# Three more score blocks turned by DMA, keys turned two groups at a time, and a written table of extra products

## The chip, the cores and the metric

The kernel runs on one core of a Trainium2 chip. The metric is the device time of one launch in microseconds (us). Three runs of the kernel before gave a median of 765.36 us (765.35 to 765.82).

Five engines work side by side, each with its own queue of instructions in order. TensorE (PE, with its weight loads shown as PEld) multiplies matrices and writes the result to PSUM. VectorE (DVE), ScalarE (ACT) and GpSimd (POOL) work on elements. SyncE (SP) only issues DMAs here: loads of `u`, stores of the output, and all transposes that the DMA engines make ("turns").

## The reference

For each of 8 batches, with S = 3200 tokens, D = 256, and 64 columns in `z`, `w_q` and `w_k`:

```
scores = (z @ z.T) / S                 # S x S, symmetric
attn   = max(scores, 0) ** 2           # symmetric too
x      = u * (attn @ v)                # S x D
q, k   = x @ w_q, x @ w_k              # S x 64
mixed  = (q @ k.T / 8) @ x             # S x D
out    = max(mixed, 0) @ w_out
```

The kernel computes `mixed` as `q @ (k.T @ x) / 8`; `k.T @ x` is the small matrix that the code calls "heads".

## The kernel before, in words

**Groups and tiles.** The 25 row tiles of 128 tokens of a batch are put into 7 groups: six of 512 tokens and a last one of 128 (`LASTG`). For each group, the transposed attention matrix is needed in blocks of 128 rows x 512 columns. One block is a score product (`scores`, L291: 64 rows of `z` against 512 columns), a first stage that scales and clamps it (`first_stage`, DVE at L305 or ACT at L303) and a second stage that squares it to fp16 (`second_stage`, POOL at L316 or ACT at L314). Blocks are made two at a time, as "score pairs": a pair fills one PSUM tile of 128 x 1024, its two matmuls use 64 rows of the array each and run side by side. Three such PSUM tiles exist (`pps`); mixes, output products and key projections use them too.

**Turned blocks.** `attn` is symmetric, so the block of groups (gi, gj) is the transpose of that of (gj, gi). Where `is_turned(gi, gj)` holds, the block is computed once, and a DMA transpose of the finished fp16 pair (`tt<-at`, issued by SP at L335) makes its mirror image. Before, ten blocks of a batch are turned: the neighbours up to two groups apart, and (0, 4). The mirror images live in seven buffers `tt0` to `tt6`, given out by a plan in which the one that comes free first is taken.

**Second product.** For each group, PE adds up `attn @ v` over all 25 row tiles in two PSUM banks, `acc0` and `acc1` (L353, 64 rows of the array per matmul in two lanes). There is one copy of these banks, so a new group's products can begin when the group before has been read out of them. That is done by `gate`: DVE multiplies one half by `u` (L491, into `x_sb`), ACT copies the other half out (L490, `gt`) and POOL multiplies it.

**Steps.** The order of all work is written by a loop over steps `k`, with three score pairs made in a step, or two and a mix. The step also takes some rows of the second product of the current group (`rows_`), which may be freshly made blocks of at least two steps ago (`LAG`) or mirror images that wait in `left`. A step that begins a group first issues a number of score pairs (`heading`) and then the group's products; the others are interleaved between the products at the shares in `shares_of`.

**Extra products.** A step can carry one of three kinds of extra work: a key step (`keys_and_heads`: project a group's `x` by `w_q` and `w_k`, copy the result out at L528, turn the keys by DMA, L535, and add up the heads of an earlier group), a mix (`mix`, L641: two matmuls of 512 columns, clamped on ACT at L662), and an output product (`project`, 16 matmuls of 256 columns, scaled on ACT at L723, stored by SP at L724). Which step carries which is decided by the rules `mix_due` and `key_due` and in the test for `projecting`, but for 15 steps that `chosen` sets by hand.

**What SP issues.** In order of the program: turns of `x` (`turn_x`, L502), loads of `u` (L179), turns of score pairs (L335), turns of keys (L535), of `z` for the next batch (`turn_z`, L160), and stores.

Of the kernel before, what the change touches and what calls it, by code (L numbers as in the profile page):

```python
# [16 lines left out]
def kernel(  # L17
# [15 lines left out]
    P = 128  # L33
# [155 lines left out]
    kxs = [pk.tile([P, 4, 2, dh], FP16, tag=f"kx{i}", name=f"kx{i}") for i in range(4)]  # L189
    raw = {}  # L190

# [34 lines left out]
    FOR_SMALL = (3, 4, 5)  # L226

# [40 lines left out]

    tt_of, tt_free = {}, [(-1.0, n) for n in range(7)]
    for b, gi, tis in tiles:  # L270
# [201 lines left out]
    def gate(b, gi):  # L472
        nn = widths[gi] // P
        if gi < LASTG:
            xs[b, gi] = px.tile([P, 4, D], FP16, tag="x_sb", name="x_sb")
        else:
            xs[b, gi] = px.tile([P, 1, D], FP16, tag="xl", name="xl", bufs=1)
        x = xs[b, gi][:].rearrange("p n d -> p (n d)")
        ug = us.pop((b, gi))[:].rearrange("p n d -> p (n d)")
# [16 lines left out]
    def turn_x(b, gi):  # L496
        nn = widths[gi] // P
        if gi < LASTG:
            xTs[b, gi] = pxt.tile([P, 4, ND, P], FP16, tag="xT_sb", name="xT_sb")
        else:  # L500
            xTs[b, gi] = pxt.tile([P, 1, ND, P], FP16, tag="xTl", name="xTl", bufs=1)
        nc.sync.dma_start_transpose(  # L502
            out=xTs[b, gi][:, 0:nn, :, :].rearrange("p n a s -> p (n a) s"),
            in_=xs[b, gi][:, 0:nn, :].rearrange("p n d -> p (n d)"),
        )


# [14 lines left out]
    def projections_out(b, gi, out):  # L522
        gw = widths[gi]
        if gi < LASTG:
            qks[b, gi] = pq.tile([P, W], FP16, tag="qk", name="qk")
        else:
            qks[b, gi] = pq.tile([P, P], FP16, tag="ql", name="ql", bufs=2)
        nc.scalar.copy(out=qks[b, gi][:, 0:gw], in_=out)  # L528

    def turn_keys(b, gi):  # L530
        gw = widths[gi]
        mine = slice(0, dh) if swapped(gi) else slice(dh, P)
        kxs.append(kxs.pop(0))
        ks[b, gi] = kxs[-1]
        nc.sync.dma_start_transpose(  # L535
            out=ks[b, gi][:, 0 : gw // P, 0, :],
            in_=qks[b, gi][mine, 0:gw],
        )

    def swapped(gi):  # L540
        return gi % 2 == 1 or gi == LASTG
# [237 lines left out]
    def between(k, fn):  # L779
        todo_between.append((k, fn))  # L780

    def group_done(k, b, gi):
        if gi < LASTG - 1:
            between(k + (5 if b + 1 < B else 3), lambda: keys_and_heads(b, [gi]))
        elif gi == LASTG and b + 1 < B:
            between(k + 5, lambda: keys_and_heads(b, [LASTG - 1, LASTG]))
# [10 lines left out]
    def keys_and_heads(b, gis):  # L797
# [5 lines left out]
        aside = None  # L803
        late = len(groups) <= NG
        heads_of = keyed[: late or len(keyed) == 2]
        if late and len(keyed) == 2 and keyed[0][0] == keyed[1][0]:
            heads_of = [(keyed[0][0], keyed[0][1] + keyed[1][1])]
            keyed[:2] = heads_of
        full = len(heads_of) == 1
# [22 lines left out]
        def after():  # L832
            for gi, o in zip(gis, outs):
                projections_out(b, gi, o)
                turn_keys(b, gi)
            if full:
                hb, hgis = keyed.pop(0)
                heads_out(hb, hgis, ps)
                if hgis[-1] == LASTG:
                    mixed_at[0] = max(mixed_at[0], now[0] - 1)  # L840
                    todo_mix.extend((hb, i, db) for i in range(LASTG // 2) for db in range(ND))
                    side.append((side_mix, side_mix_out, hb))
            if aside:
                aside[1](aside[2], ps)
            keyed.append((b, gis))
            keyed_at[0] = now[0]
# [3 lines left out]
    def group_begun(k, b, gi):  # L850
# [487 lines left out]
```

## Time and profile before

| | before |
|---|---|
| median of three runs | 765.36 us |
| the profiled execution | 765.27 us |
| its span, first to last instruction | 763.5 us |
| PE busy | 753.3 us (99%), 12888 matmuls |
| POOL, ACT, DVE busy | 545.3, 526.4, 462.0 us |
| mean granted clock of PE | 0.997 |
| packets of the DMA engines | 289613, 135.88 MB |

"Busy" is the time in which an engine has at least one instruction running. Matmuls overlap, and their ends are modelled, so PE's busy time is not by itself time at its peak rate. In a timeline row the first number is the start, the second the time from the first start to the last end of the merged instructions, and `x16` their count. A name like `SPq` is an engine's issuing of DMAs, which is not counted as busy.

### The profile page before, as it was taken

The numbers are of one execution on the slowest core, as the hardware profiler recorded it, in microseconds if no ns is written. First come the engines' busy times: TensorE is split into PE (matmuls) and PEld (weight loads), VectorE is DVE, ScalarE is ACT, GpSimd is POOL, SyncE is SP. The second block draws the span as 40 slices with busy tenths as digits, with TensorE's granted clock in tenths as the row PEclk, the third lists the DMA queues.
The fourth block names the chain that finished last, engine by engine and source line by source line (L and its number), as shares of the span: only waits on it lengthen the run. The fifth ranks groups of instructions, "written<-read, shape, count | busy, mean of one in ns | idle before, by whom it ended". The sixth has DMA issues, their size and how long they took to land.

```text
span 763.5 us, 28995 instructions
## 1 busy us (share of the span) xinstructions
PE 753.3 (99%) x12888; PEld 617.9 (81%) x12888; DVE 462.0 (61%) x458; ACT 526.4 (69%) x619; POOL 545.3 (71%) x383
## 2 busy tenths in 40 slices
PE   8999999999999999999999999999999999999996
PEld 6777888888888887888888888888878888888884
DVE  7654676546755567555665557655566565755534
ACT  8666676676767676676775867658676586776555
POOL 7988797678867688675888569966698665854540
PEclk9999999999999999999999999999999999999998
DMA  9999699997999979999999979999599995798636
GB/s 193 176 191 201 104 175 175 141 181 112 183 172 205 188 146 187 201 189 171 191 195 194 210 151 150 169 201 237 105 198 204 200 209 127 170 227 188 168 74 261
DMA packets 289613, 135.88 MB, mean 178 GB/s; under 512 B 265168, under 2 KB 269648, under 8 KB 289488
## 3 DMA queue, kind: packets, MB, share of 16 engines
q1 hardware_dynamic: 279696, 117.80, 80.2%
q0 software_dynamic: 9648, 15.98, 15.3%
q8 instruction: 100, 1.64, 0.9%
q14 instruction: 25, 0.20, 0.1%
q10 hardware_dynamic: 144, 0.26, 0.1%
HBM read 59.38 MB, written 26.21 MB: 112 GB/s over the span
## 4 chain that ended last, share of the span: by engine, by line
PE 97%; DVE 2%; ACT 1%; issue 0%; DVEq 0%; ACTq 0%
PE acc L353 72%; PE sc L291 12%; PE fo L353 5%; PE qk L353 5%; PE mx L641 1%; DVE x_sb L491 1%; DVE fo L1296 0%; PE sc L965 0%; DVE g L305 0%; ACT at L314 0%; ACT g L303 0%; PE qk L594 0%; PE xtx L618 0%; PE ztp L129 0%; PE hd L628 0%
## 5 line engine op out<-in xcount | busy, mean ns | idle before, releaser
L305 DVE TENSOR_SCALAR g<-sc 128x1024 f32<-128x1024 f32 x329 | 400.6, 1224 | 240.2 <-PE sc L291 228.5
L316 POOL TENSOR_TENSOR at<-g 128x1024 f16<-128x1024 f32 x229 | 432.3, 1897 | 123.9 <-DVE g L305 100.2
L353 PE MATMUL acc<-v_sb,at 64*128 64x256 f16 (+1 forms) x7187 | 462.0, 269 | 2.2 <-DVE x_sb L491 0.5
L353 PEld LDWEIGHTS <-at 64*128 64x128 f16 (+1 forms) x7187 | 353.9, 94 | 87.6 <-PE acc L353 25.3
L314 ACT ACTIVATE at<-g 128x1024 f16<-128x1024 f32 x227 | 236.2, 1055 | 19.3 <-DVE g L305 11.8
L353 PE MATMUL acc<-v_sb,tt 64*128 64x256 f16 x2552 | 178.7, 269 | 0.0
L303 ACT ACTIVATE g<-sc 128x1024 f32<-128x1024 f32 x127 | 130.0, 1023 | 55.3 <-PE sc L291 52.3
L291 PE MATMUL sc<-zT 64*128 64x512 f16 (+1 forms) x1008 | 164.7, 356 | 0.4 <-DVE zT L135 0.3
L353 PEld LDWEIGHTS <-tt 64*128 64x128 f16 x2552 | 130.2, 94 | 14.1
L493 POOL TENSOR_TENSOR x_sb<-gt,u_sb 128x512 f16<-128x512 f32 x48 | 61.2, 1274 | 64.5 <-ACT gt L490 60.1
L662 ACT ACTIVATE rt<-mx 128x1024 f16<-128x1024 f32 x47 | 47.9, 1024 | 32.7 <-PE mx L641 32.5
L490 ACT COPY gt<-acc 128x512 f32<-128x512 f32 x48 | 28.1, 585 | 49.9 <-PE acc L353 49.9
L291 PEld LDWEIGHTS <-zT 64*128 64x128 f16 x1008 | 51.8, 94 | 8.7 <-issue 1.5
L353 PE MATMUL fo<-wo,rt 64*128 64x256 f16 (+1 forms) x696 | 57.9, 270 | 0.0
L528 ACT CAST qk<-qk 128x512 f16<-128x512 f32 x47 | 27.5, 586 | 39.5 <-PE qk L353 36.9
L353 PEld LDWEIGHTS <-rt 64*128 64x128 f16 (+1 forms) x696 | 35.5, 94 | 15.3 <-PE fo L353 6.3
L491 DVE TENSOR_TENSOR x_sb<-acc,u_sb 128x512 f16<-128x512 f32 x48 | 33.2, 691 | 20.4 <-PE acc L353 19.2
L723 ACT ACTIVATE fo<-fo 128x1024 f32<-128x1024 f32 x39 | 39.9, 1024 | 1.9 <-PE fo L353 1.7
L353 PEld LDWEIGHTS <-x_sb 64*128 64x128 f16 x672 | 29.8, 95 | 4.5 <-PE qk L353 0.9
L353 PE MATMUL qk<-kx,x_sb 64*128 64x64 f16 x672 | 32.8, 190 | 0.0
L146 POOL DMA_DIRECT2D v_sb<-in_v_dram x49 | 28.7, 586 | 0.0
L353 PE MATMUL qk<-xT_sb,wkq 64*128 64x512 f16 (+3 forms) x118 | 25.7, 326 | 0.0
(84 smaller groups left out, 249.8 us busy)
## 6 DMA issues: line engine op xcount, KB each, us to landing
u_sb<-in_u_dram SPq DMA_DIRECT2D x48, 512.0 KB, 5.4
out_dram<-fo SPq DMA_DIRECT2D x43, 512.0 KB, 3.9
v_sb<-in_v_dram POOLq DMA_DIRECT2D x43, 256.0 KB, 5.2
tt<-at SPq DMA_TRANSPOSE x162, 5.1
out_dram<-fo SPq DMA_DIRECT2D x9, 256.0 KB, 2.9
zr<-in_z_dram POOLq DMA_DIRECT2D x7, 256.0 KB, 4.2
u_sb<-in_u_dram SPq DMA_DIRECT2D x8, 128.0 KB, 4.4
zr<-in_z_dram POOLq DMA_DIRECT2D x7, 144.0 KB, 6.4
```

Of the source, the lines that this page charges most:

```text
L146: nc.gpsimd.dma_start(out=vs[b][:, n0 : n0 + nn, :], in_=rows(v, b)[:, n0 : n0 + nn, :])
L291: nc.tensor.matmul(out=sc[:, h, at : at + w], lhsT=zT[b][half : half + dqk, ds(z_at(b, h) + ti * P, P)], rhs=zT[b][half : half + dqk, ds(z ...
L303: nc.scalar.activation(out=g[:], in_=sc[:], func=RELU, scale=GSCALE)
L305: nc.vector.tensor_scalar(out=g[:], in0=sc[:], scalar1=0.0, scalar2=GSCALE, op0=AOP.max, op1=AOP.mult)
L314: nc.scalar.square(out=out, in_=g[:])
L316: nc.gpsimd.tensor_mul(out=out, in0=g[:], in1=g[:])
L353: return nc.tensor.matmul(out=self.out, lhsT=self.lhsT(rows), rhs=self.rhs(rows), start=start, stop=stop)
L490: nc.scalar.copy(out=upper[:], in_=accs[1][:])
L491: nc.vector.tensor_mul(out=x[:, 0:n], in0=accs[0][:, 0:n], in1=ug[:, 0:n])
L493: nc.gpsimd.tensor_mul(out=x[:, n : 2 * n], in0=upper[:], in1=ug[:, n : 2 * n])
L662: nc.scalar.activation(out=out, in_=ps[:], func=RELU)
L723: nc.scalar.mul(out=flat_out[:, sl], in_=part, mul=FINAL_SCALE)
```

## The change

- `is_turned` holds for (0, 3), (1, 4) and (2, 5) too: 13 blocks of a batch are turned. Their mirror images are no longer computed. Ten buffers hold turned blocks instead of seven.
- To make room, `px` goes from 7 to 6 buffers, `pxt` from 4 to 3, `pq` from 11 to 6.
- Except in the last batch, the keys of an even group and the next odd group are put side by side in one tile `kp` of 128 partitions and are turned by one DMA; the 128-token group goes with the third pair. ACT copies the half with the queries, DVE the half with the keys (a new instruction). Heads can be added only after the pair is turned.
- `x` of the last two groups shares one tile `x5` and, except in the last batch, one DMA. The turn of `z` is cut in two DMAs (7 and 6 blocks) instead of three.
- A string `EXTRAS` sets for every step which extra product it carries: `k` a key step, `p` an output product, `m` a mix, `x` a mix and an output product, `.` none. The rules are used no more.

```diff
-    px = ctx.enter_context(tc.tile_pool(name="px", bufs=7))
+    px = ctx.enter_context(tc.tile_pool(name="px", bufs=6))
...
-    pxt = ctx.enter_context(tc.tile_pool(name="pxt", bufs=4))
+    pxt = ctx.enter_context(tc.tile_pool(name="pxt", bufs=3))
...
-    pq = ctx.enter_context(tc.tile_pool(name="pq", bufs=11))
+    pq = ctx.enter_context(tc.tile_pool(name="pq", bufs=6))
...
+    ALSO = ((0,3),(0,4),(1,4),(2,5))
+
     def is_turned(gi, gj):
-        return gi < gj < LASTG and (gj <= gi + FAR or (gi, gj) == (0, 4))
+        return gi < gj < LASTG and (gj <= gi + FAR or (gi, gj) in ALSO)
...
-    tt_of, tt_free = {}, [(-1.0, n) for n in range(7)]
+    tt_of, tt_free = {}, [(-1.0, n) for n in range(10)]
...
     def gate(b, gi):
         nn = widths[gi] // P
-        if gi < LASTG:
+        if gi < LASTG - 1:
             xs[b, gi] = px.tile([P, 4, D], FP16, tag="x_sb", name="x_sb")
-        else:
-            xs[b, gi] = px.tile([P, 1, D], FP16, tag="xl", name="xl", bufs=1)
...
+        elif gi == LASTG - 1:
+            xs[b, gi] = px.tile([P, 5, D], FP16, tag="x5", name="x5", bufs=1)
+        else:
+            xs[b, gi] = xs[b, gi - 1][:, 4:5, :]
...
     def projections_out(b, gi, out):
         gw = widths[gi]
...
+        pair = gi // 2
+        if gi % 2 == 0:
             qks[b, gi] = pq.tile([P, W], FP16, tag="qk", name="qk")
-        else:
-            qks[b, gi] = pq.tile([P, P], FP16, tag="ql", name="ql", bufs=2)
-        nc.scalar.copy(out=qks[b, gi][:, 0:gw], in_=out)
+            kps[b, pair] = pk.tile([P, W + P], FP16, tag="kp", name="kp", bufs=2)
+        else:
+            qks[b, gi] = qks[b, gi - 1]
+        q, k = (slice(dh, P), slice(0, dh)) if swapped(gi) else (slice(0, dh), slice(dh, P))
+        nc.scalar.copy(out=qks[b, gi][q, :], in_=out[q, :])
+        nc.vector.tensor_copy(out=kps[b, pair][k, 0:W], in_=out[k, :])
 
     def turn_keys(b, gi):
         gw = widths[gi]
...
+        if gi % 2 == 0 and gi < LASTG or gi == LASTG - 1:
+            return
+        pair = min(gi // 2, 2)
+        n = 5 if gi == LASTG else 4
+        kx = pk.tile([P, 5, 2, dh], FP16, tag="kp2", name="kx", bufs=2)
         nc.sync.dma_start_transpose(
-            out=ks[b, gi][:, 0 : gw // P, 0, :],
-            in_=qks[b, gi][mine, 0:gw],
+            out=kx[:, 0:n, :, :].rearrange("p n a h -> p n (a h)"), in_=kps[b, pair][:, 0 : n * P]
         )
...
-            keyed.append((b, gis))
+            if b == last:
+                keyed.append((b, gis))
+            elif gis[0] % 2 == 1:
+                keyed.append((b, [gis[0] - 1]))
+                keyed.append((b, gis))
...
-            for i, n0 in enumerate((0, 5, 9)):
-                due(k + (10 if b == 0 else 6) + i, lambda n0=n0: turn_z(b + 1, n0, 5 if n0 == 0 else 4))
+            for i, (n0, nn) in enumerate(((0, 7), (7, 6))):
+                due(k + (10 if b == 0 else 6) + i, lambda n0=n0, nn=nn: turn_z(b + 1, n0, nn))
...
-    heading_more = {165: -1}
-    chosen = {
-        18: "k", 19: "p", 20: "p", 21: "m", 35: "k", 36: "p", 38: "p", 101: "p", 142: "mp",
-        147: "k", 148: "m", 149: "m", 159: "mp", 161: "p", 163: "m"
-    }
+    heading_more = {}
+    EXTRAS = (
+        "..............k.k..k.k...k.k.k..k...mk.mkpmkmpm.kpk.p.k.mkmkmppkmmkpkpkppkmm"
+        "kpkpmmkppkmmkmmkppmkpmpkmpkmk..pkmk.mkpkpmpmppmkpkmkmpkxkxxkxkxkxxkxxxxkxk.k"
+        "."
+    )
+    chosen = {k: "mp" if c == "x" else c for k, c in enumerate(EXTRAS)}
```

More of the change, by code (lines that the diff above doesn't have):

```diff
@@ L189 @@
     kxs = [pk.tile([P, 4, 2, dh], FP16, tag=f"kx{i}", name=f"kx{i}") for i in range(4)]
-    raw = {}
+    raw, kps = {}, {}
     def load_weights():
@@ L219 @@
     LASTG = NG - 1
+    ALSO = ((0,3),(0,4),(1,4),(2,5))
     def is_turned(gi, gj):
-        return gi < gj < LASTG and (gj <= gi + FAR or (gi, gj) == (0, 4))
-    FOR_SMALL = (3, 4, 5)
+        return gi < gj < LASTG and (gj <= gi + FAR or (gi, gj) in ALSO)
+    FOR_SMALL = (3,4,5)
     def group_of(ti):
@@ L496, in turn_x @@
     def turn_x(b, gi):
-        nn = widths[gi] // P
-        if gi < LASTG:
+        n0, n1 = 0, widths[gi] // P
+        if gi < LASTG - 1:
             xTs[b, gi] = pxt.tile([P, 4, ND, P], FP16, tag="xT_sb", name="xT_sb")
+            src, dst = xs[b, gi], xTs[b, gi]
         else:
-            xTs[b, gi] = pxt.tile([P, 1, ND, P], FP16, tag="xTl", name="xTl", bufs=1)
+            if gi == LASTG - 1:
+                xTs[b, gi] = pxt.tile([P, 5, ND, P], FP16, tag="xT5", name="xT5", bufs=1)
+                xTs[b, LASTG] = xTs[b, gi][:, 4:5, :, :]
+            if b < last:
+                if gi < LASTG:
+                    return
+                n0, n1 = 0, 5
+            elif gi == LASTG:
+                n0, n1 = 4, 5
+            src, dst = xs[b, LASTG - 1], xTs[b, LASTG - 1]
         nc.sync.dma_start_transpose(
-            out=xTs[b, gi][:, 0:nn, :, :].rearrange("p n a s -> p (n a) s"),
-            in_=xs[b, gi][:, 0:nn, :].rearrange("p n d -> p (n d)"),
+            out=dst[:, n0:n1, :, :].rearrange("p n a s -> p (n a) s"),
+            in_=src[:, n0:n1, :].rearrange("p n d -> p (n d)"),
         )
@@ L783, in group_done @@
         if gi < LASTG - 1:
-            between(k + (5 if b + 1 < B else 3), lambda: keys_and_heads(b, [gi]))
+            between(
+                k + (5 if b < last else 2 if gi == LASTG - 2 else 3), lambda: keys_and_heads(b, [gi])
+            )
         elif gi == LASTG and b + 1 < B:
@@ L803, in keys_and_heads @@
         aside = None
-        late = len(groups) <= NG
-        heads_of = keyed[: late or len(keyed) == 2]
+        late = b == last
         if late and len(keyed) == 2 and keyed[0][0] == keyed[1][0]:
-            heads_of = [(keyed[0][0], keyed[0][1] + keyed[1][1])]
-            keyed[:2] = heads_of
+            keyed[:2] = [(keyed[0][0], keyed[0][1] + keyed[1][1])]
+        heads_of = keyed[:1]
         full = len(heads_of) == 1
@@ L844, in after @@
                 aside[1](aside[2], ps)
-            keyed.append((b, gis))
+            if b == last:
+                keyed.append((b, gis))
+            elif gis[0] % 2 == 1:
+                keyed.append((b, [gis[0] - 1]))
+                keyed.append((b, gis))
             keyed_at[0] = now[0]
@@ L887 @@
     due(17, cast_out_weights)
[L894 to L898 removed]
+    heading_more = {}
[3 more added lines that the diff above has]
+        "."
+    )
+    chosen = {k: "mp" if c == "x" else c for k, c in enumerate(EXTRAS)}
     def mix_due(k):
```

28 lines of the change are left out of this document (23 added, 5 removed).

## The prediction, as it was put on record

> **What bounds the kernel now.** I read the page's head first, then the chain that ended last, then the busy times by stretch.
>
> ```profile
> span 763.5 us, 28995 instructions
> ...
> PE 753.3 (99%) x12888; PEld 617.9 (81%) x12888; DVE 462.0 (61%) x458; ACT 526.4 (69%) x619; POOL 545.3 (71%) x383
> ...
> q1 hardware_dynamic: 279696, 117.80, 80.2%
> ...
> PE 97%; DVE 2%; ACT 1%; issue 0%; DVEq 0%; ACTq 0%
> ```
>
> ```profile
> 300.00:400.00 100.00, 99.84 (x1760) 82.52 (x1758) 62.79 (x61) 70.03 (x82) 74.86 (x51) 1.00 1.07 188
> ```
>
> PE is busy 753.3 of 763.5 us and carries 97% of the chain; in the stretch from 300 to 400 us it is idle 0.16 us. The columns behind the five engines are the clock (1.00), the share of the DMA engines (1.07) and GB/s. Busy can hide pauses, so the timeline must show whether PE streams:
>
> ```profile
> 301.33 1.04 PE L353 MATMUL acc<-v_sb,tt 64*128 64x256 f16 x16
> 302.20 0.38 PE L291 MATMUL sc<-zT 64*128 64x512 f16 x2
> ...
> 302.43 0.61 PE L353 MATMUL acc<-v_sb,at 64*128 64x256 f16 x8
> 302.88 1.04 PE L353 MATMUL acc<-v_sb,tt 64*128 64x256 f16 x16
> 303.75 0.38 PE L291 MATMUL sc<-zT 64*128 64x512 f16 x2
> ...
> 303.97 0.60 PE L353 MATMUL fo<-wo,rt 64*128 64x256 f16 x8
> 303.98 0.69 DVE L491 TENSOR_TENSOR x_sb<-acc,u_sb 128x512 f16<-128x512 f32 x1
> 304.00 0.59 ACT L490 COPY gt<-acc 128x512 f32<-128x512 f32 x1 [1.15 <-PE acc L353]
> 304.40 0.38 PE L291 MATMUL sc<-zT 64*128 64x512 f16 x2
> ...
> 304.63 0.61 PE L353 MATMUL fo<-wo,rt 64*128 64x256 f16 x8
> 305.08 1.91 PE L353 MATMUL acc<-v_sb,at 64*128 64x256 f16 x32
> ...
> 309.25 0.59 PE L291 MATMUL sc<-zT 64*128 64x512 f16 x4
> ```
>
> It does. From start to start, sixteen products of 256 columns take 0.87 us (301.33 to 302.20, again 302.88 to 303.75), eight take 0.43 to 0.45, a score pair 0.22 or 0.23. A second pair right behind a first adds 0.21 (0.59 against 0.38). So PE works at its rate of columns, and each change of work costs about 0.02 beyond it. What counts is how many columns PE streams, and where it must wait in between.
>
> **The change part by part.** *Three more turned blocks.* Each was 4 blocks of 128 x 512, two to a pair: 3 x 4 / 2 x 8 batches = 48 score pairs go. The order of the instructions confirms it: 880 matmuls of 512 columns become 784. The price on PE is between 0.21 and the whole life of a pair:
>
> ```profile
> L316 POOL TENSOR_TENSOR at<-g 128x1024 f16<-128x1024 f32 x229 | 432.3, 1897 | 123.9 <-DVE g L305 100.2 <-issue 9.2 <-DMA tt<-at 3.8
> L305 DVE TENSOR_SCALAR g<-sc 128x1024 f32<-128x1024 f32 x329 | 400.6, 1224 | 240.2 <-PE sc L291 228.5
> ...
> L314 ACT ACTIVATE at<-g 128x1024 f16<-128x1024 f32 x227 | 236.2, 1055 | 19.3 <-DVE g L305 11.8 <-DMA tt<-at 5.1 <-POOL at L316 1.4
> ...
> L291 PE MATMUL sc<-zT 64*128 64x512 f16 x880 | 159.5, 376 | 0.4 <-DVE zT L135 0.3
> ...
> L1296 DVE TENSOR_SCALAR fo<-fo 128x512 f32<-128x512 f32 x7 | 4.6, 687 | 1.9 <-PE fo L353 1.9
> ```
>
> That is 48 x 0.21 = 10.1 us to 48 x 0.376 = 18.0 us. I take 10.2, by the rows in which other work follows at once. The number of second products does not change: turned or not, each block is multiplied. Element work falls with the pairs: by the order of the instructions 31 first stages leave DVE, 31 second stages POOL, and 17 of each ACT. These engines are not the bound, so I cost that at nothing.
>
> The Trainium skill, in "TensorE: Matmul & The Clock Gate", section "Back-to-back issue gap", gives about 216 ns for a single matmul of 512 columns, which the rows bear out, but 131 ns for one in a sustained stream. By the latter figure the 48 pairs would be worth an estimated 6.3 us.
>
> *Fewer steps.* Each step makes three pairs, so following the loop gives 150 steps in place of 165. A step has some five changes of work at 0.02, thus 0.1 us; 15 x 0.1 = 1.5 us less. The bounds are nothing and the whole wait of a weight load at a change of lanes, 25.3 us in 106 waits:
>
> ```profile
> PEld L353 <- PE acc L353: 25.3, 106, 0.3
> ...
> ACT at L314 <- DMA tt<-at: 5.1, 4, 2.7
> ...
> POOL at L316 <- DMA tt<-at: 3.8, 4, 1.3
> ```
>
> That is 0.24 each, 3.6 us for 15. I take 1.5.
>
> *The table of extra products.* The number of key steps, mixes and output products stays. What moves is the step in which they sit, and here I expect a loss. A step that begins a group can't start its products before `acc0` and `acc1` are read out by L491 (0.69 us) and L490 (0.59). Where the step carries an output product, that time is covered: from 303.75, 1.28 us of other work lies ahead of the products at 305.08, and DVE was done at 304.67. Where only three pairs lie ahead, it isn't:
>
> ```profile
> 36.90 0.81 PE L291 MATMUL sc<-zT 64*128 64x512 f16 x6
> 37.13 0.69 DVE L491 TENSOR_TENSOR x_sb<-acc,u_sb 128x512 f16<-128x512 f32 x1 [0.50 <-PE acc L353]
> 37.15 0.59 ACT L490 COPY gt<-acc 128x512 f32<-128x512 f32 x1 [1.20 <-PE acc L353]
> ...
> 37.79 0.46 PE L353 MATMUL acc<-v_sb,at 64*128 64x256 f16 x4
> ```
>
> ```profile
> 23.36 0.83 PE L291 MATMUL sc<-zT 64*128 64x512 f16 x6
> ...
> 24.40 1.36 PE L353 MATMUL acc<-v_sb,at 64*128 64x256 f16 x21 [0.20 <-DVE x_sb L491]
> ```
>
> From 36.90 to 37.79 are 0.89 us, of which three pairs fill 0.64: a wait of 0.25, hidden in busy time. At 23.36 it is 0.40. By its rules the kernel before begins 27 groups (not counting those of 128 tokens) with an output product and only 5 with three bare pairs. The new table begins 9 with an output product, 12 with three bare pairs and 10 with a mix and two pairs, which cover the same 0.64. That is 17 more bare beginnings: 17 x 0.25 = 4.3 us, and 6.8 at 0.40. If the wait is covered in a way I don't see, it is nothing. I take 4.3.
>
> *Keys by pairs.* The ACT copy at L528 stays as long, having as many columns. DVE gains 42 copies of 64 x 512 from PSUM. No row shows one; DVE's 128x512 scaling takes 0.69, which I take: 29 us, less than the 38 that its 31 lost first stages free (31 x 1.224). What hides them is DVE's idle time (39%). That cover is thin where a key step of six rows closes a group: the copy then delays L491, and the next group with it. There are three such places ahead of a bare beginning; I take 0.35 each, 1 us, between nothing and 20 closing key steps at 0.2 (4 us). The heads run one pair later, but no heads matmul is added or lost.
>
> *DMAs and SP's queue.* SP's turns, from the rows by tile and line (nanoseconds, least/median/most):
>
> ```profile
> L335 SPq DMA_TRANSPOSE tt<-at x162: 1197/1516/5062, 12.8 to 719.3; - x162
> ...
> DMA to landing us min/median/max: 2.5/5.1/10.7
> ```
>
> ```profile
> L535 SPq DMA_TRANSPOSE kx<-qk x47: 1172/1207/3774, 58.7 to 738.4; - x47
> ```
>
> ```profile
> L160 SPq DMA_TRANSPOSE zT<-zr x21: 1200/1502/2492, 45.1 to 587.6; - x21
> ```
>
> A turn costs SP some 1.2 us whether it moves a key tile of 64 KB or a score pair of 256 KB. So merging pays for adding: 48 more turned pairs (+48 x 1.5 = 73 us) against 28 fewer key turns (-34), 7 fewer of `z` (-11) and 7 fewer of `x` (-8 at the key turn's 1.2). The count of turns goes from 317 to 323, and SP has some 20 us more to issue, where the score pairs alone take it 162 x 1.5 = 243 us now. PE shows no wait for a turned tile above; only ACT and POOL wait, 8.9 us in all, for score tiles being read. Each mirror image is turned at least four steps ahead of its first product, a step being 92.8 us / 21 = 4.4:
>
> ```profile
> 272.21 2.07 PE acc L353 x38
> 365.02 2.07 PE acc L353 x38
> ```
>
> These two rows are the same place in two batches. Four steps are 17.7 us, against a landing of at most 10.7. I cost this at nothing.
>
> The Trainium skill speaks against the added turns: "DMA: Bandwidth & Descriptors", section "Latency and other measured facts", gives a DMA transpose 261 GB/s. By that, 48 x 256 KB would be an estimated 48 us more of DMA time. The trace's share of 1.07 shows that its packet times overlap, so it can't say how full the engines are.
>
> *Buffers.* The smaller pools hold longer-lived tiles, but each is rewritten in steps in which its last reader is earlier on PE's own queue, or well past. Turned buffers get tight: six of them are rewritten one step after their last product or in that very step (two before). SP then waits, with all behind it; I cost it at nothing by the same four steps.
>
> *The sum*, against the profiled execution: 765.27 - 10.2 - 1.5 + 4.3 + 1.0 = 758.9 us. The median of the runs is 0.09 above that execution, so I predict 758.9 for the median as well.
>
> **The rivals.** *The beginnings cost nothing:* another transfer of work hides the read-out, and neither 4.3 nor 1.0 is lost. Then 765.27 - 11.7 = 753.6. Against it speaks the row at 36.90.
>
> *A removed pair is worth less:* PE could have streamed half of it under its neighbours. Then 48 pairs give 48 x 0.105 = 5.0, and the time is 764.1. The spacing of 0.21 to 0.23 speaks against it. The sustained figure of "TensorE: Matmul & The Clock Gate" in the Trainium skill points the same way, with an estimated 762.8.
>
> *SP comes late (slower):* a turned buffer that is rewritten in the step of its last product holds SP for up to a step (4.4 us), and a turn behind it takes as long as the longest above (5.06 for 1.20, 3.9 us more). That is 8.3 us, against a slack of 17.7 - 10.7 = 7.0; PE would wait 1.3 us. Once a batch that is 10.4 us, and the time 769.3. It decides from 0.8 us a batch (6.4 / 8). Against it: landings of 10.7 are the extreme of 162, with a median of 5.1, and only two rewrites fall into the very step.
>
> **How the numbers follow.** A measurement of this kernel can tell about 0.2% (1.5 us) from no change. Forecast around 758.9: 0.67; beginnings free: 0.14; a pair worth less: 0.05; SP late: 0.14. Faster is the first two, 0.81; same 0.05; slower 0.14. The range reaches down to 753.3, just under the free beginnings, and up to 763.2, which takes in bare beginnings at 0.40 and a copy that costs 4 (763.2 - 758.9 = 4.3 of the 2.5 + 3.0 that both together would add); outside lie the late SP, the cheap pairs and the extreme price of 18.0 for the pairs.
>
> **What would show it.** In the profile after: 784 score matmuls and some 210 turned pairs; PE still at 99%. Right steps: about 92.0 us from batch to batch instead of 92.8; 0.25 us between three pairs and the products that follow, at beginnings without an output product. Wrong: PE waiting for `tt` (SP late), products of a beginning that follow three pairs at once (free), DVE's new copy just ahead of a late L491 (my 1.0 too small), or DMA waits of ACT and POOL grown far above 8.9 us.

## The result and the profile after

The changed kernel takes 835.94 us (median; 832.85 to 838.2 in four runs), against 765.36 before: 1.092 times as long (95% interval 1.087 to 1.096). The prediction was 758.9, with a range of 753.3 to 763.2, so it was wrong by 77 us and on the wrong side. Every time below is the median of a kernel's runs without those more than 1.5% above its fastest, and each ratio is taken to runs of the kernel before on the same chip.

The head of the page of the kernel after, its clock in 40 slices, its first DMA queue, and the chain that ended last by engine and by line:

```profile
span 836.3 us, 28636 instructions
...
PE 772.0 (92%) x12760; PEld 637.3 (76%) x12760; DVE 447.6 (54%) x469; ACT 494.5 (59%) x585; POOL 486.9 (58%) x352
...
PEclk9999998999998999989989999979999989999999
...
q1 hardware_dynamic: 329488, 130.50, 81.4%
...
PE 72%; DMA 10%; ACT 5%; DVE 4%; POOL 3%; issue 3%; SPq 2%; DVEq 0%; ACTq 0%; POOLq 0%
PE acc L355 55%; PE sc L293 7%; DMA tt<-at 5%; DMA kx<-kp 5%; PE qk L355 4%; PE fo L355 4%; POOL at L318 2%; DVE g L307 2%; ACT at L316 2%; SPq L337 1%; ACT g L305 1%; PE mx L683 1%; DVE kp L556 1%; ACT gt L494 1%; DVE x_sb L495 0%
```

PE was idle for 10 us of its span before and is for 64 us now. It carried 97% of the chain and carries 72%; the DMAs, which did not appear there, have 10%. The profiled run itself took 838.2 us, 2.3 above the median.

Who waits for turned tiles (engine, line waited for: us in total, times, longest):

```profile
PE qk L355 <- DMA kx<-kp: 37.6, 9, 8.4
POOL at L318 <- DMA tt<-at: 25.6, 9, 6.2
ACT at L316 <- DMA tt<-at: 19.1, 11, 5.9
PEld L355 <- DMA kx<-kp: 6.3, 2, 6.1
```

Before, PE waited for no turned tile at all, and POOL and ACT for 8.9 us in all. Now PE waits eleven times for the keys of a pair, 43.9 us, in the heads' matmuls. The longest, in the timeline (start, us from first start to last end, engine, line; in brackets the idle time before, with what ended it):

```profile
544.47 0.32 PE L355 MATMUL qk<-xT_sb,wqk 64*128 64x384 f16 x1
545.19 0.53 SPq L766 DMA_DIRECT2D out_dram<-fo  x1
545.83 1.50 SPq L516 DMA_TRANSPOSE xT_sb<-x_sb  x1
547.38 3.01 SPq L337 DMA_TRANSPOSE tt<-at  x2
550.49 1.24 SPq L574 DMA_TRANSPOSE kx<-kp  x1
551.78 0.57 SPq L179 DMA_DIRECT2D u_sb<-in_u_dram  x1
552.45 5.80 SPq L337 DMA_TRANSPOSE tt<-at  x3
553.21 0.32 PE L355 MATMUL qk<-kx,x_sb 64*128 64x64 f16 x3 [8.42 <-DMA kx<-kp]
```

SP issues one DMA after another with hardly a pause; the key turn has its place in that row, is issued at 550.49, and PE goes on 2.7 us later. This is the key step 104. The keys that its heads use were copied out in the key step 102, two steps before. Ahead of the last batch's own heads, the table has nine such places (steps 29, 50, 68, 78, 104, 110, 115, 125 and 139). In the kernel before, a group's heads came two key steps after its own keys, six or more steps later except in the last batch. The change also drops that rule: heads now go into the next key step (`heads_of = keyed[:1]`).

The same stretch by windows (PE busy first, after it the other engines; the last three columns are granted clock, DMA share, GB/s):

```profile
548.00:553.00 5.00, 0.00 (x0) 0.00 (x0) 0.00 (x0) 0.00 (x0) 0.00 (x0) 0.50 0.96 183
553.00:558.00 5.00, 4.79 (x58) 3.73 (x57) 1.77 (x2) 0.58 (x1) 0.00 (x0) 0.51 1.26 185
558.00:563.00 5.00, 4.94 (x81) 3.96 (x77) 3.38 (x5) 3.40 (x4) 3.18 (x3) 1.00 0.50 85
```

From 548 to 553 us all five engines stand still while the DMA share is 0.96. The granted clock falls to 0.50 and stays there for some 5 us after the wait.

The work itself is what the prediction said: the score matmuls (784 of 512 columns, and as before 128 narrow ones), and DVE's new copy of the keys (0.685 us; I took 0.69).

```profile
L293 PE MATMUL sc<-zT 64*128 64x512 f16 (+1 forms) x912 | 149.2, 359 | 9.4 <-ACT g L305 3.4 <-DVE ha L620 3.2 <-ACT zT L172 1.1
L556 DVE CAST kp<-qk 64x512 f16<-64x512 f32 x42 | 28.8, 685 | 11.0 <-ACT qk L555 10.1
```

**Where the 72.8 us of span lie.** I took each step's time, from its first matmul to the first of the next step, and subtracted its columns at 0.2133 us per 512 (two matmuls of 64 rows count as one). That is just under the 0.215 us that a score pair of the kernel before takes at least, from its start to the next matmul. What is left over, summed by kind of step:

| us | before | after |
|---|---|---|
| columns of all steps | 704.3 | 694.0 |
| left over in 55 steps that begin a group | 13.4 | 37.1 |
| left over in the other key steps (34, now 33) | 5.2 | 64.2 |
| left over in the rest (76, now 62) | 8.5 | 9.4 |

So 10.2 us of columns went, as predicted; the other key steps cost 59.0 more, the group beginnings 23.7 more. The opening and the end account for the remaining -0.5.

### The profile page after: what moved, and what is told of

It reads as the page before. It is cut to its first block, busy times and chain, and to the rows that moved or that the text cites. A ratio compares the mean times of both kernels' runs of the same rounds, so it can differ in the third digit from the quotient of the medians.

```text
span 836.3 us, 28636 instructions
## 1 busy us (share of the span) xinstructions
PE 772.0 (92%) x12760; PEld 637.3 (76%) x12760; DVE 447.6 (54%) x469; ACT 494.5 (59%) x585; POOL 486.9 (58%) x352
## 4 chain that ended last, share of the span: by engine, by line
PE 72%; DMA 10%; ACT 5%; DVE 4%; POOL 3%; issue 3%; SPq 2%; DVEq 0%; ACTq 0%; POOLq 0%
PE acc L355 55%; PE sc L293 7%; DMA tt<-at 5%; DMA kx<-kp 5%; PE qk L355 4%; PE fo L355 4%; POOL at L318 2%; DVE g L307 2%; ACT at L316 2%; SPq L337 1%; ACT g L305 1%; PE mx L683 1%; DVE kp L556 1%; ACT gt L494 1%; DVE x_sb L495 0%
## 5 line engine op out<-in xcount | busy, mean ns | idle before, releaser
L307 DVE TENSOR_SCALAR g<-sc 128x1024 f32<-128x1024 f32 x298 | 361.3, 1222 | 304.7 <-PE sc L293 295.5
L318 POOL TENSOR_TENSOR at<-g 128x1024 f16<-128x1024 f32 x198 | 373.6, 1895 | 160.7 <-DVE g L307 111.4
L355 PE MATMUL acc<-v_sb,at 64*128 64x256 f16 (+1 forms) x6419 | 427.9, 273 | 5.8 <-ACT at L316 1.7
L355 PEld LDWEIGHTS <-at 64*128 64x128 f16 (+1 forms) x6419 | 331.9, 95 | 78.5 <-PE acc L355 18.6
L316 ACT ACTIVATE at<-g 128x1024 f16<-128x1024 f32 x210 | 216.9, 1054 | 30.6 <-DMA tt<-at 19.1
L355 PE MATMUL acc<-v_sb,tt 64*128 64x256 f16 (+1 forms) x3288 | 224.4, 273 | 0.1
L355 PEld LDWEIGHTS <-tt 64*128 64x128 f16 (+1 forms) x3288 | 173.0, 95 | 18.2 <-issue 0.4
L555 ACT CAST qk<-qk 64x512 f16<-64x512 f32 x42 | 24.3, 579 | 98.6 <-PE qk L355 98.3
L355 PEld LDWEIGHTS <-x_sb 64*128 64x128 f16 x560 | 27.9, 101 | 46.5 <-issue 36.9
L355 PEld LDWEIGHTS <-rt 64*128 64x128 f16 (+1 forms) x696 | 38.5, 95 | 12.2 <-PE fo L355 1.6
L556 DVE CAST kp<-qk 64x512 f16<-64x512 f32 x42 | 28.8, 685 | 11.0 <-ACT qk L555 10.1
L355 PE MATMUL qk<-xT_sb,wqk 64*128 64x128 f16 (+3 forms) x148 | 30.9, 338 | 3.0 <-ACT g L305 3.0
```

The source lines that it names most:

```text
L307: nc.vector.tensor_scalar(out=g[:], in0=sc[:], scalar1=0.0, scalar2=GSCALE, op0=AOP.max, op1=AOP.mult)
L316: nc.scalar.square(out=out, in_=g[:])
L318: nc.gpsimd.tensor_mul(out=out, in0=g[:], in1=g[:])
L355: return nc.tensor.matmul(out=self.out, lhsT=self.lhsT(rows), rhs=self.rhs(rows), start=start, stop=stop)
L556: nc.vector.tensor_copy(out=kps[b, pair][k, 0:W], in_=out[k, :])
```

## The experiments

Two theories at first. *Late keys:* two steps are too few between a pair's copies and its heads. *Full queue:* SP's queue of turns is behind by so much that some turn is late wherever it is put. A third came up on the way: the DMA engines, not the queue, are full.

**1. Key steps one step later, in eight places (later1).**

The extra products of the steps 29, 50, 68, 78, 104, 110, 115 and 125 change places with those of the step behind.

```diff
-        "..............k.k..k.k...k.k.k..k...mk.mkpmkmpm.kpk.p.k.mkmkmppkmmkpkpkppkmm"
-        "kpkpmmkppkmmkmmkppmkpmpkmpkmk..pkmk.mkpkpmpmppmkpkmkmpkxkxxkxkxkxxkxxxxkxk.k"
+        "..............k.k..k.k...k.k..k.k...mk.mkpmkmpm.kp.kp.k.mkmkmppkmmkppkkppkmm"
+        "kppkmmkppkmmkmmkppmkpmpkmpkm.k.pkm.kmkppkmpmppmkpmkkmpkxkxxkxkxkxxkxxxxkxk.k"
```

> The changed kernel with eight letters of its table swapped with their neighbours, so that eight key steps that add up the heads of an even group two steps after that pair's keys were copied out (steps 29, 50, 68, 78, 104, 110, 115, 125) come one step later. The turns on SP's queue are the same in number. Theory late keys (SP is several us behind, the pair's turn lands only then, PE stands in front of the heads, and its clock halves): the waits of 7 to 11 us at these places go, some 57 us and a few more of half clock, so 765 to 780. Rival full queue (48 more turned pairs keep SP or the DMA engines behind everywhere): the waits move to the next reader, above 820.

It took 809.6 us (ratio 1.055, 1.050 to 1.060): in neither theory's range. Its waits:

```profile
POOL at L318 <- DMA tt<-at: 33.8, 12, 5.8
ACT at L316 <- DMA tt<-at: 23.2, 14, 6.9
PE qk L355 <- DMA kx<-kp: 21.3, 9, 8.0
PEld L355 <- DMA kx<-kp: 19.6, 6, 8.4
```

A third step gains 26 us, but 40.9 us of waits for keys are left, and those for `tt` grow from 44.7 to 57.0. Lateness alone doesn't explain that.

**2. The keys of each group turned singly (single_keys).** They lie in the pair's tile as before, but each group's half is turned in its own key step: 28 turns more.

```diff
-        if gi % 2 == 0 and gi < LASTG or gi == LASTG - 1:
-            return
...
-            out=kx[:, 0:n, :, :].rearrange("p n a h -> p n (a h)"), in_=kps[b, pair][:, 0 : n * P]
+            out=kx[:, n0:n1, slot, :], in_=kps[b, pair][mine, n0 * P : n1 * P]
```

> The changed kernel with its table, its 13 turned blocks and its order of heads, but each group's keys turned by a DMA of their own in the group's own key step, as before the change. SP issues 28 more turns. An even group's keys then leave one key step earlier. Late keys: no long wait in front of the heads, 765 to 780 in spite of the longer queue. Full queue: SP further behind, 836 or more.

One run: 810.23 us. The even group's keys are now turned a key step earlier, and PE hardly waits for them. The waits went elsewhere, though:

```profile
POOL at L318 <- DMA tt<-at: 54.5, 19, 8.5
ACT at L316 <- DMA tt<-at: 44.1, 18, 7.5
PE qk L355 <- DMA kx<-kp: 4.8, 2, 4.3
```

POOL and ACT wait 98.6 us for score tiles that late turns are still reading.

**3. Merged DMAs and small pools alone (merge_only).** Ten turned blocks and the rules of the kernel before; the pairs of keys, the merged turns of `x` and `z` and the smaller pools stay.

```diff
-    ALSO = ((0,3),(0,4),(1,4),(2,5))
+    ALSO = ((0,4),)
...
-    chosen = {k: "mp" if c == "x" else c for k, c in enumerate(EXTRAS)}
+    chosen = {
+        18: "k", 19: "p", 20: "p", 21: "m", 35: "k", 36: "p", 38: "p", 101: "p", 142: "mp",
...
```

> The changed kernel without the three blocks (ten turned as before) and with the rules and the fifteen hand-set steps of the kernel before; the merged DMAs of keys, x and z and the smaller pools stay. Key steps lie at least three steps apart by those rules. Late keys: no long wait, 764 to 769. Rival merged turns are slow in themselves (one DMA of 128 partitions lands later than two of 64): PE waits for them here too, 790 or more.

774.72 us (ratio 1.012, 1.007 to 1.018). The engines' busy times, from its page, and its one wait of PE for keys:

```profile
PE 756.1 (98%) x12888; PEld 618.7 (80%) x12888; DVE 489.0 (63%) x500; ACT 526.0 (68%) x619; POOL 545.1 (71%) x383
```

```profile
PE qk L355 <- DMA kx<-kp: 2.1, 1, 2.1
```

So this half of the change is a loss of some 1%, and the three blocks with their table make the other 61 us (835.94 - 774.72).

**4. The short lead in the kernel before (before_lag1_tight).** Heads follow in the next key step, and key steps may be two apart, which gives seven new places with a lead of two steps.

```diff
-        heads_of = keyed[: late or len(keyed) == 2]
+        heads_of = keyed[:1]
...
-            return since > 2 and (more or not todo_proj)
+            return since > 1 and (more or not todo_proj)
...
-        return since > 2
+        return since > 1
```

> The kernel before, with ten turned blocks and single key turns, but the heads of a group added up in the next key step instead of the one after, and key steps allowed two steps apart: six times the heads follow two steps behind their keys. Late keys, as a matter of distance alone: waits of 5 to 9 us at these six, 790 to 825. Full queue: SP is not behind with the old blocks, 764 to 770.

One run: 779.6 us, between the two. With ten turned blocks the short lead makes waits of PE too, but short ones (10.5 us in all, with 3.3 of PEld and 1.7 for the keys of the 128-token groups):

```profile
PE qk L353 <- DMA kx<-qk: 5.5, 3, 3.6
```

**5. Plain transfers off SP's queue (after_off_sp, later1_off_sp, before_off_sp).** ACT issues the stores, POOL the loads of `u`; little but turns is left on SP in the loop.

```diff
-        nc.sync.dma_start(out=us[b, gi][:, 0:nn, :], in_=rows(u, b)[:, n0 : n0 + nn, :])
+        nc.gpsimd.dma_start(out=us[b, gi][:, 0:nn, :], in_=rows(u, b)[:, n0 : n0 + nn, :])
...
-            b, gi, src, [(False, nc.sync, widths[gi] // P)]
+            b, gi, src, [(False, nc.scalar, widths[gi] // P)]
```

> The changed kernel with the stores of output products issued by ACT and the loads of u by POOL, instead of by SP. SP loses some 100 DMAs of 0.5 to 0.6 us, about 57 us; the DMA engines move the same bytes. Theory SP's queue (one queue issues every turn, at a mean of 1.8 us each, and is behind for tens of us in each batch): keys land earlier, the waits in front of the heads shrink, below 800. Rival DMA engines (they are full, and SP only stands behind them): no change, 825 to 840.

> The same move of stores and loads in the kernel whose eight key steps come one step later (809.6 measured). SP's queue: what was left of the waits goes as well, 758 to 775, near the time forecast without waits. DMA engines: 800 to 815, as without the move.

> The kernel before with the same move of stores and loads. Its SP is behind too, but nothing waits for it. Both theories: 763 to 768; a loss above 770 would be the price of issuing on ACT and POOL.

All three became slower: after 883.05 us (ratio 1.154, 1.145 to 1.162), with the later keys 871.08 (1.138, 1.135 to 1.141), before 791.44 (1.033, 1.027 to 1.039). In the kernel before, whose turns stand in the prediction at 1197/1516/5062 ns and whose landings at 2.5/5.1/10.7 us, they became:

```profile
L335 SPq DMA_TRANSPOSE tt<-at x162: 1232/1835/7199, 13.2 to 745.5; - x162
...
DMA to landing us min/median/max: 3.0/5.7/19.1
```

Taking 102 transfers (56 loads, 46 stores) off the queue made the turns on it longer; their mean rose from 1.83 to 2.23 us. I read this so: what one queue had kept apart now ran side by side and shared the DMA engines. The Trainium skill says in "DMA: Bandwidth & Descriptors", section "Rules for kernel authors", that spreading DMAs over SP, ACT and GpSimd brings no bandwidth, since all run on the same 16 DMA engines. Here it did harm. That it is the DMA engines and not something else in the queues is argued, not shown. In the kernel before, the move also costs POOL 0.56 us for issuing each load, and POOL's waits for `tt` grow from 3.8 to 58.8 us; the two effects were not separated.

**6. Fewer bytes (short_stores).** Each store of four row tiles writes only its first.

```diff
-                out=rows(out, b)[:, n0 + at : n0 + at + n, :],
+                out=rows(out, b)[:, n0 + at : n0 + at + 1, :],
...
```

> The changed kernel that stores only the first 128 tokens of each 512 (the output leaves out the rest): the same number of DMAs on SP, but 43 stores of 128 KB for 512 KB. SP's queue: no change, 820 to 840. DMA engines: some 39 us less for each engine, and with it most of the delay, below 810.

One run: 825.32 us. That is some 10 us less (7.5 below the fastest run of the kernel after), with PE's waits for keys at 36.9 us instead of 43.9. By this one run the bytes of the stores matter a little; they are not the bound.

**7. The key turns on a queue of their own (keys_by_act, later1_keys_by_act).**

```diff
-        nc.sync.dma_start_transpose(
+        nc.scalar.dma_start_transpose(
             out=kx[:, 0:n, :, :].rearrange("p n a h -> p n (a h)"), in_=kps[b, pair][:, 0 : n * P]
```

> The kernel after, with the turn of a pair's keys issued on ACT's queue; all other turns and transfers stay on SP's. If the heads wait because the key turn stands behind other turns in SP's queue, the nine waits of 8.4 us for it go, and with them most of the half clock behind them: some 50 to 60 us less, 775 to 790 us, with the waits for tt (25.6 us on POOL) not longer than they were. If the turn is late because its own work is late (the two copies, or two steps being too few for any turn), the waits stay at more than 6 us each and the time is 825 to 840. If turns on two queues get in each other's way, as the transfers moved off SP did, all turns become longer than their mean of 1.8 us and the time is over 845.

> The kernel after with eight key steps one step later and the turn of a pair's keys on ACT's queue. If the place in SP's queue is what made the waits move to other steps when the keys came later (809.6 us), this lies below both edits alone, at 765 to 780 us. If what is short is the rate at which all turns can be carried out, whatever the queue, it stays at 800 to 815. If turns on two queues hinder each other, over 815.

946.65 us (ratio 1.236, 1.234 to 1.238) and 940.65 (1.229, 1.225 to 1.232). This isn't what I meant to test, as the trace of keys_by_act shows: first ACT's rows around one key turn, then the semaphore waits of ACT's queue at the turn's line (x79: least/median/most in ns), then the waits on SP's queue.

```profile
575.87 0.58 ACT L555 CAST qk<-qk 64x512 f16<-64x512 f32 x1 [1.36 <-PE qk L355]
586.16 1.21 ACTq L574 DMA_TRANSPOSE kx<-kp  x1
587.42 0.38 ACT L808 ACTIVATE fs<-qk 128x256 f32<-128x256 f32 x1 [10.96 <-issue]
```

```profile
L574 ACTq EVENT_SEMAPHORE  x79: 17/38/8302, 76.6 to 848.2; - x79
```

```profile
SPq L516 <- DMA kx<-kp: 39.8, 9, 7.7
SPq L337 <- DMA kx<-kp: 37.9, 9, 7.8
```

The program that is built orders the turns of the two queues: ACT's waits until SP's have landed, SP's next waits until ACT's has landed. In the trace, each of the 21 key turns starts 0.1 to 0.3 us (once 2.6) after the last of SP's turns has landed. ACT does nothing for 11 us, and the queue of turns loses its overlap. The Trainium skill asks for this order in "DMA: Bandwidth & Descriptors", section "Silent corruption: two transposing streams in flight at once": the later stream's first transpose has to wait for the earlier stream's full completion. The trace agrees that it is kept, at 77.7 us of such waits on SP. So ordered, a second queue relieved the first of nothing.

**8. The waits filled with matmuls (filled).** Is it the half clock that costs?

```diff
+        if now[0] in (29, 50, 68, 78, 104, 125):
+            for _ in range(28):
+                nc.tensor.matmul(out=outs[0], lhsT=zeros[:], rhs=wo[:].rearrange("p a d -> p (a d)"), start=True, stop=True)
```

> The kernel after with 28 more matmuls of 512 columns (28 x 0.21 = 6 us), of operands that are long there, at the beginning of each of six key steps (29, 50, 68, 78, 104, 125) whose heads wait 7 to 11 us; their products are overwritten. They stand in the time that was waited in any case. If the granted clock falls because PE is idle there, and the stretches at half clock behind six waits cost some 2.4 to 3.4 us each, the time falls by 12 to 20 us, to 816 to 824 us, although PE has 36 us more to do. If the half clock costs nothing, or has another cause, it stays at 832 to 840. If the waits are not there in those steps, the 36 us come on top: 860 to 872.

838.21 us (ratio 1.094, 1.088 to 1.099): no change against 835.94. The clock from its page, the added matmuls by line, and its waits of PE for keys:

```profile
PEclk9999999999999999999999999999999999999999
```

```profile
L848 PE MATMUL qk<-wo,zeros 128*128 128x512 f16 x168 | 37.3, 379 | 0.0
```

```profile
PE qk L355 <- DMA kx<-kp: 10.5, 7, 2.4
```

No slice of the clock is below 9 any more, and 37.3 us of matmuls went into the waits at no cost: with them in it, the six steps together are 5.7 us shorter (0.9 a wait), where I had expected 12 to 20. Even that didn't show in the time: later steps waited longer, step 139 alone by 3.2 us, where the lead is two steps and nothing was filled in. PE was waiting there in any case.

**9. Without the turns of the three blocks, without the wait for the keys, without either (no_block_turns, keys_not_awaited, neither).** The products and every step stay.

```diff
 # no_block_turns
+            if (gi, gj) in ((0, 3), (1, 4), (2, 5)):
+                continue
...
+        if (gj, gi) in ((0, 3), (1, 4), (2, 5)):
+            return ident[rows, :]
 # keys_not_awaited
-                    rhs=lambda r, gi=gi, n=n: ks[b, gi][r, n, 0, :],
+                    rhs=lambda r: wo[r, 0, 0:dh],
```

> The kernel after without the turns of its three extra blocks: 48 fewer on SP's queue (275 instead of 323), every matmul, copy and step as it was; the second products that would read those blocks read a constant tile, so that part of the output is not computed. The pairs' keys are still needed two steps after their copies. If what makes the heads wait is the length of SP's queue, 48 x 1.8 = 86 us of it are gone, the key turns are no longer behind it, and the time is 755 to 775 us, where the prediction had it. If the two steps are too few whatever the queue, the nine waits stay and it is 820 to 838. In between, 785 to 815, both count.

> The kernel after, in which the heads of all batches but the last read a constant tile in place of the turned keys: every turn is still issued and every matmul done, but nothing waits for the turn of a pair's keys, and the heads come out as another product. If the short lead of the keys is the whole loss, 43.9 us of waits and their half clock go and the time is 765 to 785 us. If SP's queue cannot keep up with PE, the waits move to the score blocks' tiles (POOL and ACT on tt, 44.7 us in the profile after, grow to 70 or more) and the time is 795 to 815. Below 765, PE is paid all that the 48 score pairs gave up.

> The two edits together: no turns of the three extra blocks, and heads that read a constant tile in place of the turned keys, so that neither the queue nor the short lead can hold PE. Everything else is the kernel after. If the loss is the sum of those two and of longer group beginnings, this takes off no_block_turns (788.0) only what its key steps still lose, some 10 us: 775 to 780, and what is then above the predicted 758.9 is the price of the beginnings, some 15 to 20 us. If the two were the whole loss, it is 757 to 763. If some queue still holds PE, 785 or more.

| | us | ratio to before |
|---|---|---|
| after | 835.94 | 1.092 (1.087 to 1.096) |
| without the 48 turns | 787.96 | 1.028 (1.024 to 1.033) |
| keys not awaited | 794.79 | 1.038 (1.034 to 1.042) |
| neither | 776.85 | 1.015 (1.013 to 1.017) |

Waits of no_block_turns, and then of keys_not_awaited:

```profile
PE qk L357 <- DMA kx<-kp: 8.6, 7, 2.2
```

```profile
POOL at L318 <- DMA tt<-at: 59.3, 21, 6.2
ACT at L316 <- DMA tt<-at: 37.8, 18, 6.4
```

With 48 turns fewer, the same short lead costs 11.1 us (787.96 - 776.85) and no wait for keys exceeds 2.2 us. With the full queue and no wait for keys, 17.9 us are lost (794.79 - 776.85), by score tiles that stay occupied. Together they cost 59.1. So neither theory was right alone: the long waits need both, a queue that is behind and a turn that is needed two steps later. And a third part is left, since neither still takes 18 us more than predicted.

**10. One score pair fewer ahead of the products of 17 group beginnings (neither_spread).**

```diff
-    heading_more = {}
+    heading_more = dict.fromkeys((20, 24, 30, 34, 51, 53, 56, 60, 64, 75, 86, 90, 94, 105, 117, 126, 128), -1)
```

> The kernel neither, with one score pair fewer ahead of the second products at 17 group beginnings that have no output rows or keys in their step; that pair comes among the second products instead. If such a beginning is long because its last score pair waits for one of the three PSUM tiles, the wait goes and the time falls by 5 to 9 us (17 x 0.3 to 0.5). If it is long because the accumulators are still being copied out, less work stands ahead of the first product, the wait only changes its place, and the time stays within 2 us or rises by up to 5.

774.28 us (ratio 1.012, 1.010 to 1.014), 2.6 less. The profiled executions differ by 3.3 in span, 3.0 of it before the loop's first step (15.2 and 12.2 us from the start). Over the 55 beginnings, 34.8 us are left over in the one and 34.5 in the other: no difference. One beginning in the timelines of neither and then of neither_spread:

```profile
420.17 0.69 DVE L560 CAST kp<-qk 64x512 f16<-64x512 f32 x1
420.23 0.44 PE L687 MATMUL mx<-qk,hs 64*128 64x512 f16 x2
420.45 0.44 PE L293 MATMUL sc<-zT 64*128 64x512 f16 x2
...
420.89 0.29 DVE L624 TENSOR_TENSOR ha<-ha,qk 128x128 f32<-128x128 f32 x1
...
421.10 0.68 DVE L499 TENSOR_TENSOR x_sb<-acc,u_sb 128x512 f16<-128x512 f32 x1
...
421.24 0.39 PE L293 MATMUL sc<-zT 64*128 64x512 f16 x2 [0.35 <-DVE ha L624]
...
421.83 0.61 PE L357 MATMUL acc<-v_sb,at 64*128 64x256 f16 x8 [0.21 <-DVE x_sb L499]
```

```profile
416.97 0.44 PE L687 MATMUL mx<-qk,hs 64*128 64x512 f16 x2
...
417.83 0.68 DVE L499 TENSOR_TENSOR x_sb<-acc,u_sb 128x512 f16<-128x512 f32 x1
...
418.57 0.83 PE L357 MATMUL acc<-v_sb,at 64*128 64x256 f16 x12 [0.95 <-DVE x_sb L499]
```

From the mix to the first product are 1.60 us in both. In the first, PE waits 0.35 for the PSUM tile of the key step and 0.21 for the accumulators; in the second, with one pair fewer ahead, 0.95 for the accumulators alone. What sets it in this place is DVE: the key copy, the addition of the heads and only then L499, one behind the other.

In all beginnings, PE's waits of over 0.15 us sum to 8.8 us for PSUM tiles and 1.7 for the accumulators in neither, and to 7.0 and 7.5 in neither_spread: the wait changes its place. The largest ones in neither (all of them are in beginnings):

```profile
PE qk L357 <- ACT g L305: 4.5, 3, 2.1
PE sc L293 <- DVE ha L624: 1.4, 4, 0.4
```

The first row is of three beginnings that carry a key step themselves: its PSUM tile comes free only when ACT's first stage has read the score pair in it. The kernel before has no such wait, and neither_spread left these three as they were. By kind, what is left over per beginning:

| | before | neither |
|---|---|---|
| with an output product | 33 x 0.19 | 14 x 0.36 |
| with a key step | 13 x 0.25 | 14 x 0.73 |
| with neither of the two | 9 x 0.44 | 27 x 0.72 |

No version among these beats the kernel before.

## Why the prediction was wrong

**The turned blocks and the steps: right.** The 48 score pairs took 10.2 us of columns with them, and the steps that begin no group and carry no keys lost 1.2 us less in neither than before (7.3 against 8.5), where 1.5 was forecast for fewer steps. Against a cheaper pair, the second rival, speaks the spacing: of 435 score pairs in the trace before, none takes less than 0.215 us from its start to the next matmul, with a median of 0.216. That a pair that goes gives back this time was not measured singly. The first, free beginnings, is refuted by what the beginnings lost.

**Keys by pairs: the step that failed.** "The heads run one pair later, but no heads matmul is added or lost" counted the matmuls and priced no wait. Nor do the heads come later, counted from the turn: the kernel before leaves six steps or more from a group's turn to its heads for 44 of the 49 groups ahead of the last batch, and three for another 3; the new one leaves two or three for 19. The even group of a pair can be turned only when the odd group's keys are there, and its heads then go into the very next key step, in nine places two steps on. What the prediction asked of each `tt` (how many steps from turn to first product?) it did not ask of `kx`. The profile after shows eleven waits of 43.9 us there, and the key steps outside group beginnings 59.0 us longer.

**DMAs and SP's queue: priced at nothing, wrongly.** "PE shows no wait for a turned tile" was read as slack in the queue. The sum of the issue times was right: all turns take SP 533 us before and 551 after, 18 more where some 20 was forecast. And the queue was as busy already: SP issues for up to 71 us without a pause of 0.2 us before, and for up to 68 after. The slack existed only because the kernel before asks for nothing soon. The runs put the turns' part at 48.0 us (835.94 against 787.96), of which most needs the short lead as well. The Trainium skill's 261 GB/s, from which the prediction estimated 48 us more DMA time, pointed at this part; that the two numbers agree proves nothing, since the 48.0 are time lost in waits, not time of the DMA engines.

**The rival "SP comes late" had the right engine and the wrong place.** It put the wait at `tt`, rewritten in the step of its last product, 1.3 us a batch and 769.3 in all. It came at `kx`, up to 8.4 us at a time. Score tiles (`at`) came second: POOL and ACT wait 44.7 us for turns to finish reading them instead of 8.9, a sign that the prediction had named.

**The table's beginnings and DVE's copy: right mechanism, wrong size.** I took 4.3 + 1.0 = 5.3 us; with queue and keys out of the way it is 34.8 - 13.4 = 21.4. The count of bare beginnings was right: 18 more, or the 17 forecast without the 128-token groups. The price was not: I took 0.25 from one place (0.40 at another), and 27 of them lose 0.72 each. That price held only the wait ahead of the first product; the bare beginnings of the kernel before lose 0.44 each over the whole step. The beginnings with a key step I left out: their number hardly changes, but they lose 7.1 us more, 4.5 of it in the row for ACT's first stage above. I looked for key copies ahead of a late L491 in three places; in neither, 14 beginnings without an output product follow a key step, at 0.78 each (before: three, at 0.27). The 27 others lose 0.69, so a key copy just ahead isn't the main difference. Of the 21.4, the pairs' copies and buffers have a part under the old table too: in merge_only the beginnings lose 18.6 us, 5.2 more than before.

**The sum as it should have been:** 765.3 - 10.2 (columns) - 1.2 (fewer steps) + 21.4 (beginnings) = 775.3 for neither, which took 776.85, in the profiled execution with 3.0 us in a longer opening (and 774.28 with the other heading); the keys' short lead with a short queue +11.1, the queue without it +17.9, and 30.1 because the two meet. The first sum is bookkeeping: what the columns don't explain counts as left over, so it has to close nearly. The three parts behind it are differences of runs. Even without any DMA wait, the change costs more at the beginnings than it saves in columns.

What stays open: why a turn takes 1.2 us in one place and 5 in another. The plain transfers beside it may be part of it (experiment 5); the causes were not separated. Of the 21.4 us, the rows of experiment 10 show the waits for PSUM tiles and accumulators; how much each of DVE's copy, its addition of heads and the table's key steps has was not tested singly.

## What to carry to other kernels

An in-order queue with no visible wait isn't one with slack: ask of every transfer in it how soon the change will need it, not only of those that the change adds. Merging two transfers into one delays the first to the second's readiness, so follow its earliest reader. Price an uncovered wait by counting what stands ahead of the copy on its own engine at each place, not by the cheapest example.

## What I had not expected of the hardware

- Moving plain DMAs from the turns' queue to other engines' queues made the turns longer (median 1.52 to 1.84 us, landing at most 10.7 to 19.1), and the kernel before 3.3% slower; why was not separated (experiment 5).
- The granted clock fell to half in six of PE's waits for keys (4.3 to 8.4 us long), 2.9 to 4.9 us after PE had stopped, and stayed there for 4.3 to 6.0 us after PE went on. The Trainium skill describes such a fall after about 3.4 us of idleness ("TensorE: Matmul & The Clock Gate", section "What's actually happening"); the trace agrees roughly: in the wait shown above, PE stopped at 544.8 us, and in windows of 1 us the clock is 1.00 up to 547 and 0.50 from 548 on. Filling the waits kept the clock full there and gained nothing.
- All 21 key turns on ACT's queue, issued when no other turn was in flight, took 1.21 to 1.30 us to issue and landed after a median of 2.4 us, as the fastest on SP (1.20 and 2.5) did. On SP in the kernel after, the same turns took up to 3.1 us and landed after a median of 4.5.
